# Fixed buffers for the transposed keys, and a finer last transfer, in a decode attention kernel

## The chip, the cores and the metric

The kernel runs on one core of a Trainium2 chip. The metric is the device time of one execution in microseconds (us); the medians, the lowest and the highest run are given. A profile has its own clock, the *span*, from the first to the last instruction of the core. The device time is a little longer than the span, and that little gets a name, *the time outside the span*.

TensorE does the matmuls (PE in the profile, PEld its weight loads), VectorE (DVE) the transposes and small vector work, ScalarE (ACT) activations, GpSimd (POOL) masks, and SyncE (SP) issues the loads.

## The reference, cut to what matters

```python
x = A_x                                        # [4, 1, 1024]
g = sigmoid((x * gate_w).sum(-1))
a = attention(x @ wq, k_cache, v_cache) @ wo   # 4 x 32 heads, 8192 keys of 128 each
b = x + sigmoid(x @ w_r) * ((silu(x @ w_gate) * (x @ w_up)) @ w_down)
return g * a + (1 - g) * b
```

There is one query per head. Keys and values are 268 MB each, every byte is used once, and nearly all of the time is their loading.

## The kernel before

Each step `u` handles two heads. A 4 MB piece of keys comes into one of five ring slots; VectorE transposes it in four chunks into a tile `T` from a pool of two; TensorE multiplies the chunk. The matching 4 MB piece of values comes eight steps later into the same ring and is read by TensorE only.

```python
ring = ctx.enter_context(tc.tile_pool(name="ring", bufs=5))
ttp = ctx.enter_context(tc.tile_pool(name="ttp", bufs=2))
# ... cut ...
def k_piece(u):
    # ... cut: the query's weights Z ...
    kn = slot()                                                # 128 rows of 32 KB
    nc.sync.dma_start(out=kn[:], in_=kv_view(A_k_cache, u))
    for c in range(JR // CJ):                                  # 4 chunks
        T = ttp.tile([P, CJ, 2, 32, 2], BF, name="T", tag="T")
        nc.vector.transpose(out=T[:].rearrange("p j h i e -> p (j h i e)").bitcast(U32),
                            in_=kn[:, c * CJ * Dh:(c + 1) * CJ * Dh].bitcast(U32))
        for he in range(4):
            for z in range(2):
                nc.tensor.matmul(sps[:, z, :], lhsT=Z[:, he, s:s + P], rhs=T[:, 16 * z:16 * z + 16, half, :, e], ...)
```

Dependencies are found by the framework, which also places the waits on semaphores. When a tile of the pool is used again, VectorE's new write waits for TensorE's last read of it and, besides, for VectorE's own earlier write.

At the end, after the last value piece, the output projection's weights `wo` come in 1 MB blocks; the last two blocks come in halves, and each half is multiplied as it lands:

```python
def wo_block(g, r0=0, r1=FR):                   # FR = 4 rows per partition, of 2 KB each
    # ... cut ...
    nc.sync.dma_start(out=w[:, r0:r1]..., in_=wov[:, g, r0:r1]...)
    def use():
        for r in range(r0, r1):
            for n in range(NH):                 # 2 matmuls a row
                mm_acc(acc[:, n * NB:(n + 1) * NB], LT[:, r, g, :], w[:, r, n * NB:(n + 1) * NB])
    return use
# ... cut ...
last += [wo_block(g, r, r + FR // 2) for g in (NWB - 2, NWB - 1) for r in (0, FR // 2)]
```

Of the kernel before, what the change touches and what calls it, by code (L numbers as in the profile page):

```python
# [9 lines left out]
BF = mybir.dt.bfloat16  # L10
F32 = mybir.dt.float32
U32 = mybir.dt.uint32
ACT = mybir.ActivationFunctionType
ALU = mybir.AluOpType
# [25 lines left out]
def kernel(  # L40
# [23 lines left out]
    nc = tc.nc  # L64
    P = 128
    Bn, Sq, D = A_x.shape
    _, H, Sk, Dh = A_k_cache.shape
    F = B_w_gate.shape[1]
    DT = D // P
# [10 lines left out]
    CJ = 32  # L80
    NT = Bn * H // HT
    LAG = GT
    FR = 4
# [9 lines left out]

    const = ctx.enter_context(tc.tile_pool(name="const", bufs=1))
    ring = ctx.enter_context(tc.tile_pool(name="ring", bufs=5))
    ttp = ctx.enter_context(tc.tile_pool(name="ttp", bufs=2))
    ptp = ctx.enter_context(tc.tile_pool(name="ptp", bufs=1))
    stat = ctx.enter_context(tc.tile_pool(name="stat", bufs=2))
    accp = ctx.enter_context(tc.tile_pool(name="accp", bufs=1, space=PSUM))
# [5 lines left out]
    def small(shape, dtype=F32):  # L105
        return mps.tile(shape, dtype, name="small", tag="small")

    def slot():
        return ring.tile([P, RING], BF, name="piece", tag="piece")


    NX = Bn + 2
    x6 = const.tile([NX, D], BF)
# [5 lines left out]
    acc4 = accp.tile([P, 2, 512], F32)  # L119
    o_ps = accp.tile([P, 2, 512], F32)  # L120
    q_ps = scp.tile([P, 2, 512], F32, name="S_ps")
# [15 lines left out]
    for he in range(4):  # L137
        half, e = divmod(he, 2)
# [48 lines left out]
    def mm_acc(out_ap, lhsT, rhs, start=False):  # L187
        nc.tensor.matmul(out_ap, lhsT=lhsT, rhs=rhs, start=start, stop=True, skip_group_check=True)  # L188
# [3 lines left out]

    def gates():
        rg_ps = small([P, 2, Bn])
        wrep = ttp.tile([P, 2, DT, P], BF, name="wrep", tag="T")
        for i in range(2):
            nc.vector.tensor_copy(out=wrep[:, i, :, :], in_=xw[:, :, Bn + i:Bn + i + 1].to_broadcast([P, DT, P]))
            for t in range(DT):
                nc.tensor.matmul(rg_ps[:, i, :], lhsT=wrep[:, i, t, :], rhs=xT[t], start=(t == 0), stop=(t == DT - 1))
        nc.scalar.activation(out=sgb[:], in_=rg_ps[:], func=ACT.Sigmoid)  # L200
        nc.vector.tensor_scalar(out=c12[:, 0, :], in0=sgb[:, 1, :], scalar1=-1.0, scalar2=1.0, op0=ALU.mult, op1=ALU.add)
        nc.vector.tensor_tensor(out=c12[:, 1, :], in0=c12[:, 0, :], in1=sgb[:, 0, :], op=ALU.mult)
        nc.vector.tensor_tensor(out=dg[:], in0=ident[0:Bn, 0:Bn], in1=c12[0:Bn, 0, :], op=ALU.mult)

    def add_x():
        xf = ttp.tile([Bn, D], F32, name="xf", tag="T")
        nc.vector.tensor_copy(out=xf[:], in_=x6[0:Bn])
        for n in range(NH):
            mm_acc(acc[:, n * NB:(n + 1) * NB], dg[:], xf[:, n * NB:(n + 1) * NB])

# [17 lines left out]
    def wq_piece(t0):  # L228
        w = slot()[:, :TW * H * Dh].rearrange("p (t n) -> p t n", t=TW)
        nc.sync.dma_start(out=w, in_=wqv[:, t0:t0 + TW, :])  # L230
        x_rows(q_ps, w, t0, H * Dh // NB)

    def q_done():
        qs = ttp.tile([P, 2, 4, P], BF, name="qs", tag="T")
        nc.vector.tensor_copy(out=qs[:].rearrange("p z c d -> p z (c d)"), in_=q_ps[:])
        qt = small([P, 2, 4, 4, 32], BF)
        for z in range(2):
            for c in range(4):
                nc.tensor.transpose(out=qt[:, z, c].rearrange("p k i -> p (k i)"), in_=qs[:, z, c, :], identity=identb[:])
            nc.vector.tensor_copy(out=qT[:, 16 * z:16 * z + 16, :].rearrange("p (k c) b -> p c k b", c=4),  # L240
                                  in_=qt[:, z, :, :, 0:Bn])
        qa_ps = small([P, 4, H * Bn])
        for he in range(4):
            nc.tensor.matmul(qa_ps[:, he, :], lhsT=R[:, he, :], rhs=qT[:].rearrange("p h b -> p (h b)"),
                             start=True, stop=True)
        nc.vector.tensor_copy(out=qa[:].rearrange("p e h b -> p e (h b)"), in_=qa_ps[:])
# [4 lines left out]
        x_rows((o_ps, acc4)[w_i], w, t0, FG)  # L251

    def h_done():
        h = ttp.tile([P, 2, 512], F32, name="h", tag="T")
        nc.scalar.activation(out=h[:], in_=o_ps[:], func=ACT.Silu)
        nc.vector.tensor_tensor(out=h[:], in0=h[:], in1=acc4[:], op=ALU.mult)
        for z in range(2):
            ht = small([P, FR, 4, 32])
            for r in range(FR):
                nc.tensor.transpose(out=ht[:, r].rearrange("p k i -> p (k i)"), in_=h[:, z, r:512:FR], identity=ident[:])  # L260
            kn = min(4, FG - 4 * z)
            for r in range(FR):
                nc.vector.tensor_tensor(out=hT[:, 4 * z:4 * z + kn, r, :], in0=ht[:, r, 0:kn, 0:Bn],
                                        in1=c12[:, 1:2, :].to_broadcast([P, kn, Bn]), op=ALU.mult)
# [12 lines left out]
    NWB = H // WB  # L277
# [13 lines left out]
    def wo_block(g, r0=0, r1=FR):  # L291

        home, at = divmod(g, 4)
        if home not in wo_home:
            wo_home[home] = slot().rearrange("p (g r n) -> p g r n", g=4, r=FR)
        w = wo_home[home][:, at]
        nc.sync.dma_start(out=w[:, r0:r1].rearrange("p r n -> p (r n)"),
                          in_=wov[:, g, r0:r1].rearrange("p r n -> p (r n)"))

        def use():  # L300
            for r in range(r0, r1):
                for n in range(NH):
                    mm_acc(acc[:, n * NB:(n + 1) * NB], LT[:, r, g, :], w[:, r, n * NB:(n + 1) * NB])
        return use
# [6 lines left out]
    def flush():  # L311
        while pending:
            pending.pop(0)()

    def heads(u):
        return divmod(u * HT, H)

    def kv_view(cache, u):
        b, h0 = heads(u)
        return cache[b, h0:h0 + HT].rearrange("h (r j) d -> (h r) (j d)", j=JR)  # L320

    def k_piece(u):
        b, h0 = heads(u)
        g, t = divmod(u, GT)
        Z = Zt[u % 2]
        nc.gpsimd.tensor_tensor(out=Z[:, :, 31:31 + P].rearrange("p e (s d c) -> p e s d c", s=HT, d=QH)[:, :, :, :, 0],  # L326
                                in0=qa[:, :, h0:h0 + HT, b:b + 1].to_broadcast([P, 4, HT, QH]),
                                in1=mq[:].rearrange("p o (s d) -> p o s d", s=HT).to_broadcast([P, 4, HT, QH]), op=ALU.mult)
        if t == 0:
            S_ps[g] = scp.tile([P, 2, 512], F32, name="S_ps")  # L330
        sps = S_ps[g]
        kn = slot()
        nc.sync.dma_start(out=kn[:], in_=kv_view(A_k_cache, u))
        for c in range(JR // CJ):
            T = ttp.tile([P, CJ, 2, 32, 2], BF, name="T", tag="T")
            nc.vector.transpose(out=T[:].rearrange("p j h i e -> p (j h i e)").bitcast(U32),  # L336
                                in_=kn[:, c * CJ * Dh:(c + 1) * CJ * Dh].bitcast(U32))
            s = 31 - (JT * t + c)
            for he in range(4):
                half, e = divmod(he, 2)  # L340
                for z in range(2):
                    nc.tensor.matmul(sps[:, z, :], lhsT=Z[:, he, s:s + P], rhs=T[:, 16 * z:16 * z + 16, half, :, e],  # L342
                                     start=(t == 0 and c == 0 and he == 0),
                                     stop=(t == GT - 1 and c == JT - 1 and he == 3))
            if c == 0:
                flush()
        if t == GT - 1:
            softmax(g)
# [35 lines left out]
    def v_piece(u):  # L384
# [31 lines left out]
        def finish():  # L416
# [8 lines left out]


    gates()
    wq_piece(0)
    wq_piece(TW)
    q_done()  # L430
    side = [lambda: gu_piece(wgv, 0, 0), lambda: gu_piece(wgv, 0, TW), lambda: gu_piece(wuv, 1, 0),
            lambda: (gu_piece(wuv, 1, TW), h_done()), lambda: wd_piece(0, 4), lambda: wd_piece(4, FG - 4)]
    GE = NWB - RH // WB
    order = []
# [3 lines left out]
    for kind, u in order:  # L438
        if kind == "k":
            k_piece(u)  # L440
        if (kind, u) == ("v", NT - 1):
            for g in range(2):
                wo_block(g)()
        if kind == "v":
            v_piece(u)
        if side and (kind == "v" or u < LAG):
            side.pop(0)()
        if (kind, u) == ("k", NT // 2):
            add_x()
        if (kind, u) == ("v", NT - RT):  # L450
            o_rows(0, GE)
    last = [wo_block(g) for g in range(2, NWB - 2)]
    last += [wo_block(g, r, r + FR // 2) for g in (NWB - 2, NWB - 1) for r in (0, FR // 2)]
    last.pop(0)()
    flush()
    last.pop(0)()
# [38 lines left out]
```

## Time and profile before

| | before |
|---|---|
| device time, median of 3 (lowest to highest) | 1349.41 us (1349.39 to 1349.46) |
| span of the profiled run | 1347.8 us |
| moved | 576.2 MB at a mean 428 GB/s |
| busy: TensorE, VectorE | 79%, 47% |

From the page of the kernel before: the row of DMA busy tenths and of GB/s in 40 slices of the span, then two of the queues (packets, MB, share of the 16 DMA engines' span).

```profile
DMA  9999999999999999999999999999999999999997
GB/s 403 433 433 422 433 430 430 432 433 430 430 433 430 430 431 434 429 431 432 433 428 432 433 430 430 433 431 429 432 434 429 428 433 434 429 428 434 432 423 323
...
q1 hardware_dynamic: 22104, 575.68, 99.5%
q8 instruction: 27, 0.44, 0.1%
```

The loads never pause: 9 in every slice but the last. This kernel is bound by its loads.

Next, the view of line 336, the key transposes, before. The last number of a waiting line is how often.

```profile
L336 DVE STREAM_TRANSPOSE T<-piece x256: 2253/2271/2314, 33.1 to 1232.9; 128x2048 uint32<-128x2048 uint32 x128
L336 DVEq EVENT_SEMAPHORE  x230: 21/21/50, 35.5 to 1230.8; - x115
its engine sat idle before it (us, times) until:
  DMA piece<-in_A_k_cache_dram: 321.1, 45
  PE S_ps L342: 106.4, 62
  PE o_ps L401: 9.1, 1
```

VectorE's idle time before a transpose is ended by a load or by TensorE, never by VectorE itself. The second row is the waits that did not fit into a transpose and became instructions of their own, of 21 ns. (The `x115` at its end, as the `x128` of the first row, is the view's count of forms.)

Two rows of VectorE's timeline before (start, us, what). The four transposes of the first row, by the order of instructions, carry the wait on VectorE itself; the two of the second do not.

```profile
611.51 8.89 DVE L336 STREAM_TRANSPOSE T<-piece 128x2048 uint32<-128x2048 uint32 x4 [8.33 <-DMA piece<-in_A_k_cache_dram]
...
636.50 4.44 DVE L336 STREAM_TRANSPOSE T<-piece 128x2048 uint32<-128x2048 uint32 x2
```

Both come to 2.22 us a transpose.

The end of the chain that ended last, before: start, us, what.

```profile
1328.82 14.95 DMA piece<-in_A_wo_dram
1343.77 0.04 issue
1343.81 1.04 PE acc L188 x4
1344.85 0.02 issue
1344.87 0.57 ACT res L463
```

The last load lands at 1343.77, four matmuls take 1.04 us, then come the casts and the stores.

### The profile page before, as it was taken

How to read it: one execution, taken by the hardware profiler on the slowest of the kernel's cores; microseconds unless marked ns; L12 is line 12 of the kernel's file. 1: busy time of each engine (PE TensorE's matmuls, PEld its weight loads, DVE VectorE, ACT ScalarE, POOL GpSimd, SP SyncE). 2: the span in 40 equal slices, each digit the busy share in tenths (PEclk: the TensorE clock that was granted, in tenths of full speed). 3: DMA queues.
4: the chain of work that ended last, by engine and by line, in shares of the span. 5: the costliest groups of instructions: out<-in, count | busy, mean ns of one | idle time of the engine just before them, and what ended most of it. 6: DMA issues, size and time to landing. Idle time of an engine off the chain costs nothing.

```text
span 1347.8 us, 8253 instructions
## 1 busy us (share of the span) xinstructions
PE 1059.3 (79%) x4600; PEld 233.2 (17%) x2412; DVE 631.4 (47%) x375; ACT 41.5 (3%) x46; POOL 47.9 (4%) x115
## 2 busy tenths in 40 slices
PE   2667779876978868876998769888788859797878
PEld 0111111211111111111212111211112112121111
DVE  3555755535544554454545454444544456346000
ACT  0000010001000010001000010000000010000000
POOL 2000000000000000000000000000000000000000
PEclk8878989898989989989898879899888979999899
DMA  9999999999999999999999999999999999999997
GB/s 403 433 433 422 433 430 430 432 433 430 430 433 430 430 431 434 429 431 432 433 428 432 433 430 430 433 431 429 432 434 429 428 433 434 429 428 434 432 423 323
DMA packets 22162, 576.22 MB, mean 428 GB/s; under 512 B 2399, under 2 KB 2407, under 8 KB 2925
## 3 DMA queue, kind: packets, MB, share of 16 engines
q1 hardware_dynamic: 22104, 575.68, 99.5%
q8 instruction: 27, 0.44, 0.1%
q14 instruction: 11, 0.08, 0.0%
q10 hardware_dynamic: 20, 0.02, 0.0%
HBM read 575.68 MB, written 0.01 MB: 427 GB/s over the span
## 4 chain that ended last, share of the span: by engine, by line
DMA 50%; PE 30%; DVE 11%; issue 6%; ACT 1%; POOL 1%; SPq 0%; DVEq 0%; ACTq 0%
DMA piece<-in_A_k_cache_dram 40%; PE o_ps L401 16%; PE S_ps L342 13%; DVE T L336 10%; DMA piece<-in_A_v_cache_dram 9%; PE small L419 1%; DMA piece<-in_A_wo_dram 1%; POOL PB L373 1%; DVE PT L367 1%; ACT PTs L365 1%; ACT OS L411 1%; DVE OS L412 1%; POOL tot L377 0%; PE acc L188 0%; PE o_ps L225 0%
## 5 line engine op out<-in xcount | busy, mean ns | idle before, releaser
L336 DVE STREAM_TRANSPOSE T<-piece 128x2048 uint32<-128x2048 uint32 x256 | 576.1, 2288 | 437.0 <-DMA piece<-in_A_k_cache_dram 321.1
L342 PE MATMUL S_ps<-T,Z 128*128 128x512 bf16 x2048 | 544.6, 416 | 246.6 <-DVE T L336 235.3
L401 PE MATMUL o_ps<-piece,PB 128*16 128x512 bf16 x2048 | 457.6, 382 | 14.8 <-DMA piece<-in_A_v_cache_dram 14.8
L342 PEld LDWEIGHTS <-Z 128*128 128x128 bf16 x1024 | 108.0, 105 | 667.2 <-issue 664.3
L401 PEld LDWEIGHTS <-PB 128*16 128x16 bf16 x1024 | 91.9, 90 | 373.1 <-issue 361.3
L412 DVE SCALAR_TENSOR_TENSOR OS<-o_ps,mE,OS 128x512 f32<-128x512 f32 x16 | 12.0, 751 | 174.6 <-ACT OS L411 174.6
L326 POOL TENSOR_TENSOR Z<-qa,mq 128x16 bf16<-128x16 bf16 x64 | 16.7, 262 | 1072.3 <-PE S_ps L342 1054.3
L411 ACT ACTIVATE OS<-o_ps,mE 128x512 f32<-128x512 f32 x16 | 11.0, 687 | 1040.5 <-PE o_ps L401 1040.5
L419 PEld LDWEIGHTS small<-selg,OS 128*128 128x128 f32 x128 | 24.9, 273 | 12.2 <-issue 11.1
L419 PE MATMUL small<-selg,OS 128*128 128x8 f32 x128 | 22.3, 302 | 0.0
L353 DVE TENSOR_REDUCE m<-S_ps 128x1 f32<-128x1024 f32 x8 | 9.8, 1225 | 15.9 <-PE S_ps L342 15.9
L188 PE MATMUL acc<-piece,LT 128*4 128x512 bf16 x64 | 14.9, 378 | 1.7 <-DMA piece<-in_A_wo_dram 1.6
L373 POOL COPY PB<-PT 64x1024 bf16<-64x1024 bf16 x8 | 15.1, 1884 | 29.1 <-DVE rex L375 29.1
L372 ACT COPY PB<-PT 64x1024 bf16<-64x1024 bf16 x8 | 15.3, 1908 | 10.6 <-DVE PT L367 10.6
L367 DVE STREAM_TRANSPOSE PT<-PTs 128x1024 bf16<-128x1024 bf16 x8 | 10.0, 1245 | 11.9 <-ACT PTs L365 11.9
L188 PE MATMUL acc<-piece,hT 128*4 128x512 bf16 x56 | 12.4, 379 | 0.0
L131 PE MATMUL small<-identb,x 6*128 6x6 bf16 x8 | 0.6, 194 | 14.2 <-DVE identb L128 14.2
L379 DVE RECIPROCAL rinv<-tot 128x16 f32<-128x16 f32 x8 | 2.0, 253 | 19.9 <-POOL tot L377 19.9
L365 ACT ACTIVATE PTs<-S_ps,negm 128x1024 bf16<-128x1024 f32 x8 | 8.9, 1113 | 70.0 <-DVE negm L362 70.0
L225 PE MATMUL S_ps<-piece,xw 128*4 128x512 bf16 x64 | 6.6, 591 | 3.0 <-DMA piece<-in_A_wq_dram 3.0
L422 DVE SCALAR_TENSOR_TENSOR OT<-small,sgb,rinv 128x8 bf16<-128x8 f32 x16 | 3.2, 202 | 11.7 <-PE small L419 11.7
L358 POOL PARTITION_ALL_REDUCE gmx<-mex x8 | 3.1, 390 | 81.9 <-issue 50.3
(72 smaller groups left out, 74.6 us busy)
## 6 DMA issues: line engine op xcount, KB each, us to landing
piece<-in_A_k_cache_dram SPq DMA_DIRECT2D x64, 4096.0 KB, 39.4
piece<-in_A_v_cache_dram SPq DMA_DIRECT2D x63, 4096.0 KB, 39.1
piece<-in_A_wq_dram SPq DMA_DIRECT2D x2, 4096.0 KB, 22.1
piece<-in_B_w_gate_dram SPq DMA_DIRECT2D x2, 3584.0 KB, 40.1
piece<-in_B_w_up_dram SPq DMA_DIRECT2D x2, 3584.0 KB, 34.6
piece<-in_A_wo_dram SPq DMA_DIRECT2D x6, 1024.0 KB
piece<-in_B_w_down_dram SPq DMA_DIRECT2D x1, 4096.0 KB, 35.6
piece<-in_A_v_cache_dram SPq DMA_DIRECT2D x4, 1024.0 KB, 32.6
```

The lines of the kernel that those rows point to most:

```text
L188: nc.tensor.matmul(out_ap, lhsT=lhsT, rhs=rhs, start=start, stop=True, skip_group_check=True)
L326: nc.gpsimd.tensor_tensor(out=Z[:, :, 31:31 + P].rearrange("p e (s d c) -> p e s d c", s=HT, d=QH)[:, :, :, :, 0], in0=qa[:, :, h0:h0 + HT ...
L336: nc.vector.transpose(out=T[:].rearrange("p j h i e -> p (j h i e)").bitcast(U32), in_=kn[:, c * CJ * Dh:(c + 1) * CJ * Dh].bitcast(U32))
L342: nc.tensor.matmul(sps[:, z, :], lhsT=Z[:, he, s:s + P], rhs=T[:, 16 * z:16 * z + 16, half, :, e], start=(t == 0 and c == 0 and he == 0), ...
L365: nc.scalar.activation(out=PTs[:], in_=sps[:].rearrange("p z n -> p (z n)"), func=ACT.Exp, bias=negm[:, 0:1], scale=scale, accum_out=rs[:, ...
L367: nc.vector.transpose(out=PT[:].rearrange("p j i -> p (j i)"), in_=PTs[:])
L372: nc.scalar.copy(out=Bv[0:W, :, :, 0, :], in_=Pv[0:W])
L373: nc.gpsimd.tensor_copy(out=Bv[W:P, :, :, 1, :], in_=Pv[W:P])
L401: nc.tensor.matmul(o_ps[row:row + NM, e, :], lhsT=B_[:, JT * t + c, z, w].rearrange("p e s j -> p (e s j)"), rhs=vn[:, j0 * Dh:(j0 + 4) * ...
L411: nc.scalar.activation(out=o_sb[:], in_=o_ps[:, 0, :], func=ACT.Copy, scale=mE[:, 0:1])
L412: nc.vector.scalar_tensor_tensor(out=o_sb[:], in0=o_ps[:, 1, :], scalar=mE[:, 1:2], in1=o_sb[:], op0=ALU.mult, op1=ALU.add)
L419: nc.tensor.matmul(oT[:, :], lhsT=o_sb[:, q * Dh:(q + 1) * Dh], rhs=selg[:, q].rearrange("p t s -> p (t s)"), start=(q == 0), stop=(q == 3))
```

## The change

Its intent is twofold: take away VectorE's waits on itself (two fixed buffers, and a declaration to the framework that a transpose need not wait for the one two before it, because that one's readers are waited for anyway), and shorten the work behind the last load (the last block in three transfers, the last of one row per partition). Core of the diff; the other users of the old pool were moved to the fixed buffers in the same way and are cut:

```diff
-    ttp = ctx.enter_context(tc.tile_pool(name="ttp", bufs=2))
+    Tt = [const.tile([P, CJ * P], BF, name=f"T{i}") for i in range(2)]
+    turned = []
+
+    def turn(in_ap):
+        T = Tt[len(turned) % 2]
+        i = nc.vector.transpose(out=T[:].bitcast(U32), in_=in_ap.bitcast(U32)).ins
+        if len(turned) >= 2:
+            tc.declare_no_dep(i, turned[-2], reason="its readers are waited for")
+        turned.append(i)
+        return T[:].rearrange("p (j h i e) -> p j h i e", j=CJ, h=2, i=32)
...
-            T = ttp.tile([P, CJ, 2, 32, 2], BF, name="T", tag="T")
-            nc.vector.transpose(...)
+            T = turn(kn[:, c * CJ * Dh:(c + 1) * CJ * Dh])
...
-    last += [wo_block(g, r, r + FR // 2) for g in (NWB - 2, NWB - 1) for r in (0, FR // 2)]
+    last += [wo_block(NWB - 2, 0, 2), wo_block(NWB - 2, 2, 4)]
+    last += [wo_block(NWB - 1, 0, 2), wo_block(NWB - 1, 2, 3), wo_block(NWB - 1, 3, 4)]
```

More of the change, by code (lines that the diff above doesn't have):

```diff
@@ L194, in gates @@
         rg_ps = small([P, 2, Bn])
-        wrep = ttp.tile([P, 2, DT, P], BF, name="wrep", tag="T")
+        wrep = Tt[0][:, 0:2 * DT * P].rearrange("p (w t d) -> p w t d", w=2, t=DT)
         for i in range(2):
@@ L205, in add_x @@
     def add_x():
-        xf = ttp.tile([Bn, D], F32, name="xf", tag="T")
-        nc.vector.tensor_copy(out=xf[:], in_=x6[0:Bn])
+        xf = Tt[len(turned) % 2][0:Bn, 0:2 * D].bitcast(F32)
+        nc.vector.tensor_copy(out=xf, in_=x6[0:Bn])
         for n in range(NH):
@@ L233, in q_done @@
     def q_done():
-        qs = ttp.tile([P, 2, 4, P], BF, name="qs", tag="T")
-        nc.vector.tensor_copy(out=qs[:].rearrange("p z c d -> p z (c d)"), in_=q_ps[:])
+        qs = Tt[1][:, 0:1024].rearrange("p (z c d) -> p z c d", z=2, c=4)
+        nc.vector.tensor_copy(out=qs.rearrange("p z c d -> p z (c d)"), in_=q_ps[:])
         qt = small([P, 2, 4, 4, 32], BF)
@@ L253, in h_done @@
     def h_done():
-        h = ttp.tile([P, 2, 512], F32, name="h", tag="T")
-        nc.scalar.activation(out=h[:], in_=o_ps[:], func=ACT.Silu)
-        nc.vector.tensor_tensor(out=h[:], in0=h[:], in1=acc4[:], op=ALU.mult)
+        h = Tt[len(turned) % 2][:, 0:2048].bitcast(F32).rearrange("p (z n) -> p z n", z=2)
+        nc.scalar.activation(out=h, in_=o_ps[:], func=ACT.Silu)
+        nc.vector.tensor_tensor(out=h, in0=h, in1=acc4[:], op=ALU.mult)
         for z in range(2):
@@ L334, in k_piece @@
         for c in range(JR // CJ):
-            T = ttp.tile([P, CJ, 2, 32, 2], BF, name="T", tag="T")
-            nc.vector.transpose(out=T[:].rearrange("p j h i e -> p (j h i e)").bitcast(U32),
-                                in_=kn[:, c * CJ * Dh:(c + 1) * CJ * Dh].bitcast(U32))
+            T = turn(kn[:, c * CJ * Dh:(c + 1) * CJ * Dh])
             s = 31 - (JT * t + c)
```

## The prediction

> **What bounds the kernel.** The loads do. The page counts 576.2 MB at a mean 428 GB/s over a span of 1347.8 us; its DMA row shows 9 in every slice but the last, and in windows of 10 us the sixteen DMA engines are busy 0.95 to 1.05 of the time from 10 to 1330 us, without a gap. [...] VectorE is busy 47%, TensorE 79%, both fed by the loads. The queue is deep: a 4 MB piece lands 39 us after its issue, though it takes 9.8 us at 428 GB/s, so some four are in flight.
>
> **What the change removes.** By the order of instructions, 239 of the 256 key transposes wait on VectorE's own semaphore before; three do after. Waits on TensorE and the loads stay. I expect almost nothing:
> - The waits view lists as enders of VectorE's idle time before transposes only the key loads (321.1 us), the score matmuls (106.4) and the value matmuls (9.1): never VectorE. The own wait is for a transpose two back, long done.
> - Four transposes that carry it run in 8.89 us; two that don't, in 4.44 us: 2.22 us each. [...]
> - 115 separate semaphore instructions of 21 ns go, 2.4 us in sum, on an engine half idle.
> - Were a transpose 0.1 us earlier, its slot would go back 0.1 us earlier to a queue holding some 30 us of work: off the critical path.
>
> The order on TensorE and of the loads before the tail is unchanged.
>
> **The tail.** After the last load (1343.8 us) come four matmuls (1.04 us), casts (0.6) and stores. The change leaves two matmuls behind the last piece; at the trace's 0.21 us a matmul and 0.38 for the last, about 0.6 us: 0.43 us saved. Against it: one more transfer, with rows of 2 KB for 4 KB. The DMA rate falls before the end (246, 207, 45 GB/s in windows of 2 us from 1338), so some DMA engines finish up to 5 us before the last; the split doesn't mend that. [...] Tail transfers wait at issue for a semaphore used eight transfers before (27.3 us of such waits): the new last one waits for a wo piece landing near 1331 us, 12 us before the end, so the queue shouldn't run dry.
>
> **Predicted time:** 1348.9 us, 0.3 to 0.5 below before; 8 in 10: 1346.8 to 1350.6. Faster by over 2%: 0.005; within 2%: 0.99; slower by over 2%: 0.005.
>
> **What would show it.** Right: mean 427 to 429 GB/s; transposes still 2.22 us apart, with the same enders of idle time, each within 10 us of now; separate semaphore instructions on VectorE near zero; two matmuls after the last load, about 0.6 us; the last load ending within 1 us of 1343.8. Wrong: a gap in the DMA row, another DMA rate, or TensorE's wait for transposes (235.3 us) falling by tens of us with the span following.
>
> **What would make it wrong.** Drift of the load rate between runs [...]; the last transfer issued late or landing slowly on a lagging DMA engine; own waits hiding a cost that the view puts down to TensorE.

The forecast's sum came to 0.3 to 0.5 us saved, 1348.9 us. Of its two terms, the 0.43 us saved in matmuls stands; the other, an allowance against it for the extra transfer, was a guess without a number of the trace behind it. That the loads bound the kernel rests on the measured DMA row and rate, and that the own waits cost nothing on the measured 2.22 us a transpose with and without them.

## The result, and the profile after

| | before | after |
|---|---|---|
| device time, median of 6 (lowest to highest) | 1349.40 us (1349.26 to 1349.46) | 1349.52 us (1349.23 to 1349.70) |
| span of the profiled run | 1347.8 us | 1347.4 us |
| ratio, 95% interval | | 1.0001, 0.9988 to 1.0014 |

A ratio is the mean time of one kernel's fast runs over that of the other's fast runs of the same rounds, so it is not quite the ratio of the medians. The expected third to half of a microsecond is missing, and the two rows of the table disagree: the span is 0.4 us shorter, the device time is not. Which of the two is right is the question of the experiments.

First, the profile after. From the page of the changed kernel:

```profile
DMA  9999999999999999999999999999999999999997
...
q1 hardware_dynamic: 22248, 575.68, 99.5%
q8 instruction: 27, 0.44, 0.1%
```

The view of the key transposes, now line 117:

```profile
L117 DVE STREAM_TRANSPOSE T<-piece x256: 2253/2271/2312, 32.8 to 1233.0; 128x2048 uint32<-128x2048 uint32 x128
L117 DVEq EVENT_SEMAPHORE  x49: 21/21/50, 51.7 to 1224.9; - x49
its engine sat idle before it (us, times) until:
  DMA piece<-in_A_k_cache_dram: 309.9, 42
  PE S_ps L352: 122.4, 65
  PE acc L200: 3.2, 1
```

The separate waits fell from 230 to 49. The idle time before transposes is what it was (435.5 us by these rows, 436.6 before), some 10 us of it moved from loads to TensorE. VectorE's timeline after:

```profile
611.40 8.89 DVE L117 STREAM_TRANSPOSE T<-piece 128x2048 uint32<-128x2048 uint32 x4 [9.40 <-DMA piece<-in_A_k_cache_dram]
...
636.71 4.44 DVE L117 STREAM_TRANSPOSE T<-piece 128x2048 uint32<-128x2048 uint32 x2
```

To the hundredth of a microsecond the same. The end of the chain after:

```profile
1326.22 16.20 DMA piece<-in_A_wo_dram
1342.42 0.04 issue
1342.46 1.91 PE acc L200 x8
1344.37 0.02 issue
1344.40 0.57 ACT res L474
```

TensorE now runs the last eight matmuls of `wo` without a pause, and is done at 1344.37 in place of 1344.85. The completion records in the trace put the landing of the very last load at 1343.73, against 1343.77 before: the loads end where they ended, and the work behind them is 0.6 us in place of 1.1. So within the span the tail did just what was predicted. The chain shows one thing more: it runs through the landing of the transfer before the last (1342.42), not of the last. TensorE came from six matmuls straight to its last two at 1343.77, 0.04 us after the last landing, so here the last load and TensorE's own work end together, and no run shows that a still finer split would gain anything.

### The profile page after: what moved, and what is told of

Its sections match the earlier page's. It is cut to its first block, busy times and chain, and to the rows that moved or that the text cites. A ratio compares the mean times of both kernels' runs of the same rounds, so it can differ in the third digit from the quotient of the medians.

```text
span 1347.4 us, 8079 instructions
## 1 busy us (share of the span) xinstructions
PE 1065.2 (79%) x4600; PEld 234.8 (17%) x2412; DVE 631.7 (47%) x375; ACT 41.5 (3%) x46; POOL 48.0 (4%) x115
## 4 chain that ended last, share of the span: by engine, by line
DMA 48%; PE 30%; DVE 17%; issue 2%; ACT 1%; POOL 1%; SPq 0%; DVEq 0%; ACTq 0%
DMA piece<-in_A_k_cache_dram 41%; DVE T L117 15%; PE o_ps L411 14%; PE S_ps L352 14%; DMA piece<-in_A_v_cache_dram 5%; DMA piece<-in_A_wo_dram 1%; PE small L429 1%; POOL PB L383 1%; ACT PTs L375 1%; DVE PT L377 1%; DVE OS L422 1%; ACT OS L421 0%; DVE m L363 0%; PE acc L200 0%; POOL tot L387 0%
## 5 line engine op out<-in xcount | busy, mean ns | idle before, releaser
L117 DVE STREAM_TRANSPOSE T<-piece 128x2048 uint32<-128x2048 uint32 x256 | 576.2, 2288 | 436.0 <-DMA piece<-in_A_k_cache_dram 309.9
L338 POOL TENSOR_TENSOR Z<-qa,mq 128x16 bf16<-128x16 bf16 x64 | 16.8, 263 | 1072.7 <-PE S_ps L352 1053.2
L200 PE MATMUL acc<-piece,hT 128*4 128x512 bf16 x56 | 12.4, 379 | 0.0
```

What stands on the lines that cost most here:

```text
L117: i = nc.vector.transpose(out=T[:].bitcast(U32), in_=in_ap.bitcast(U32)).ins
L200: nc.tensor.matmul(out_ap, lhsT=lhsT, rhs=rhs, start=start, stop=True, skip_group_check=True)
L338: nc.gpsimd.tensor_tensor(out=Z[:, :, 31:31 + P].rearrange("p e (s d c) -> p e s d c", s=HT, d=QH)[:, :, :, :, 0], in0=qa[:, :, h0:h0 + HT ...
```

## The experiments

Eleven experiments were run. The differences below are of a few tenths of a microsecond, and the 95% interval of a ratio is about 0.0013 wide to each side (1.8 us), so no interval alone separates them. What does is that the runs of one kernel on one chip mostly scatter by 0.2 to 0.4 us, and that the ranges in question don't overlap; where they do, nothing is claimed.

### The two halves of the change, alone

The changed kernel again, then the fixed buffers with the old tail, then the new tail with the old pool, all on one chip. The edits are the two hunks above, one at a time.

> The changed kernel once more, beside its two halves on one chip. Theory (loads bound it; the own waits cost nothing; the tail split shortens the span by about 0.4 us): ratio to before 0.9995 to 1.0003. Rival (the two halves pull against each other): the ratio is also near 1, but the halves alone differ from 1 in opposite directions by over 0.0005.

> Fixed buffers alone, the tail as before. Theory: ratio 1.0000 within 0.0004; idle time of VectorE before key transposes by the same enders within 15 us of 437; span about 1347.8 us with the last load landing near 1343.8. Rival (own waits cost time, the new tail gives it back): 0.5 us or more below before.

> The three-transfer tail alone, with the pool and its own waits. Theory: the span falls by 0.3 to 0.5 us as in the profile of the changed kernel (1347.4 after 1347.8), the timed ratio 0.9996 to 1.0001. Rival (the extra transfer costs what the shorter last step saves): ratio 1.0000 or above.

| kernel (5 runs each, before 9) | device time, median (range) | span, median | outside the span (range) |
|---|---|---|---|
| before | 1349.40 us (1349.28 to 1349.59) | 1347.7 us | 1.66 to 1.76 us |
| both | 1349.40 us (1349.30 to 1349.52) | 1347.4 us | 2.00 to 2.10 us |
| fixed buffers alone | 1349.71 us (1349.64 to 1349.95) | 1347.7 us | 2.01 to 2.09 us |
| new tail alone | 1349.12 us (1349.07 to 1349.22) | 1347.4 us | 1.67 to 1.74 us |

The last column is device time less span, run by run. By their numbers all three theories held: the ratios are 1.0000, 1.0003 and 0.9998, and the rival's halves, over 0.0005 from 1, are not there. But in device time the halves have opposite signs, as the rival written for the first run had it, and each range lies clear of that of the kernel before. The tail alone gains 0.28 us of device time, all of it within the span. The fixed buffers alone lose 0.31 us, none of it within the span: there the view of their transposes shows 46 waits for loads and 62 for TensorE (45 and 62 before), and the last load lands at 1343.83. They make the time *outside* the span 0.34 us longer. Together they cancel. That is where the expected gain went.

### How far VectorE is from the critical path

Before asking why, the prediction's main claim was tested by making VectorE much slower. After each key transpose of the kernel before, one more of half the size:

```diff
+            nc.vector.transpose(out=xd[:].bitcast(U32),
+                                in_=kn[:, c * CJ * Dh:c * CJ * Dh + CJ * Dh // 2].bitcast(U32))
```

> The kernel before with one more transpose of half size after every key transpose, 256 in all, results unused; at about half of 2.22 us each, some 290 us more work on VectorE (47% busy to about 68%). Theory (VectorE is off the critical path, behind a queue of loads some 30 us deep): the time stays within 0.2%, DMA row 9 throughout. Rival (VectorE's pace reaches the time through the give-back of key slots): longer by a few per cent, up to 20%.

It took 1349.45 us (1349.24 to 1349.54, 4 runs), against 1349.40 before. From its page, first part and groups:

```profile
PE 1030.6 (76%) x4600; PEld 228.4 (17%) x2412; DVE 914.3 (68%) x631; ACT 41.6 (3%) x46; POOL 48.0 (4%) x115
...
L339 DVE STREAM_TRANSPOSE xd<-piece 128x1024 uint32<-128x1024 uint32 x256 | 308.0, 1203 | 0.0
```

308 us of added work on VectorE cost nothing that can be measured. So a change that saves VectorE a few microseconds of work cannot be expected to shorten the span.

### Does the own wait cost anything where the loads do not bound?

Both kernels (with the old tail) with thin loads: each key piece loads half its bytes and uses them twice, each value piece a quarter. The sums differ from the reference's; the comparison with the reference passed all the same, so it is not a fine one.

```diff
-        nc.sync.dma_start(out=kn[:], in_=kv_view(A_k_cache, u))
+        nc.sync.dma_start(out=kn[:, 0:RING // 2], in_=kv_view(A_k_cache, u)[:, 0:RING // 2])
...
-        for c in range(JT):        # value matmuls
+        for c in range(1):
```

> A wrong result on purpose: each key piece loads half of its bytes and uses them twice, each value piece loads and multiplies a quarter; pool and own waits as before. The loads fall to about 216 MB, 505 us at 428 GB/s, so VectorE (576 us of key transposes) and TensorE bound it: I expect 620 to 720 us. It is the reference point for the next run: does the own wait cost time where VectorE is the bound?

> The same thin loads with fixed buffers, without the own waits. Theory (the own wait is for a transpose two back, long done, and costs nothing even where VectorE bounds): within 0.3% of the run with the pool, key transposes still 2.22 us apart in a row. Rival (own waits cost tens of ns each, hidden so far behind the loads): faster by 239 times 20 to 100 ns, 5 to 24 us, 1 to 4%.

Both ran slower than the 620 to 720 us that I had expected, 835.65 us (834.58 to 836.67) with the pool and 833.57 us (832.53 to 838.12) with fixed buffers, 4 runs each: VectorE was 75% busy and TensorE 81%, so neither bounds the run alone. The medians are 0.25% apart and the ranges overlap, so the total leaves open a cost of 2 us; the 5 to 24 us of the rival are not there. The timelines answer directly. Pool, then fixed buffers:

```profile
397.96 6.65 DVE L336 STREAM_TRANSPOSE T<-piece 128x2048 uint32<-128x2048 uint32 x3
405.88 6.70 DVE L336 STREAM_TRANSPOSE T<-piece 128x2048 uint32<-128x2048 uint32 x3 [1.27 <-PE S_ps L342]
```

```profile
399.66 6.66 DVE L117 STREAM_TRANSPOSE T<-piece 128x2048 uint32<-128x2048 uint32 x3
407.58 6.70 DVE L117 STREAM_TRANSPOSE T<-piece 128x2048 uint32<-128x2048 uint32 x3 [1.27 <-PE S_ps L352]
```

In the run with the pool the first and the third of each three carry the own wait (by the semaphores in the trace; 191 of its 256 transposes do, against 3 with fixed buffers). Three in a row take 6.65 to 6.70 us with and without it. It has no cost that these rows show.

### What lengthens the time outside the span

The fixed-buffer kernels differ from the others in one thing that has nothing to do with buffers: VectorE's program is shorter, because 175 separate waits are gone from it. To tell the two apart, first 256 copies of one element were added to the fixed-buffer kernel with the old tail, then only 16 to the changed kernel. The cut below is of the second; the first has the copy after every transpose.

```diff
+            if c == 0 and u % 4 == 0:                    # 16 copies; without this line 256
+                nc.vector.tensor_copy(out=xd[:], in_=kn[:, 0:1])
```

> Fixed buffers with the old tail, and 256 copies of one element added on VectorE (results unused). In the runs so far, the device time exceeds the span of the trace by 1.70 us with the pool (before, the tail alone, the loaded VectorE) and by 2.05 us with the fixed buffers. Theory L (that part depends on how many instructions VectorE's program has: 614 records before, 692 in the loaded one, 439 with fixed buffers, about 695 here): back to 1.70 us. Theory B (it comes with the fixed buffers themselves): stays at 2.05 us. The span stays at 1347.7 within 0.3 us in both.

> The changed kernel with only 16 one-element copies added on VectorE. The device time exceeded the span by 2.05 us in every run whose VectorE program has 439 records (changed kernel, fixed buffers alone, all weight loads), and by 1.70 us at 454 (thin loads with fixed buffers), 614, 689 and 692. Theory L (the length of VectorE's program decides, with a step between 439 and 454): at about 455 records back to 1.70 us outside the span, the span 1347.4 as in the changed kernel, so 1349.1 us, 0.3 below both kernels. Rival (what the 256 copies or the thin loads did to timing inside the span brought it back): stays 2.05 us, 1349.4.

Fixed buffers with 256 copies took 1349.30 us (1349.11 to 1349.41), against 1349.46 (1349.25 to 1349.60) before on the same chip; their span, 1347.6 us, is that of the fixed buffers alone within 0.1, and the time outside it is back to 1.71: theory L. Put in order of the number of VectorE's instruction records in the trace, over all runs:

| kernel | VectorE records | outside the span (range) |
|---|---|---|
| changed (first measurement; again) | 439 | 2.03 to 2.10; 2.00 to 2.10 us |
| fixed buffers alone | 439 | 2.01 to 2.09 us |
| all weight loads (next section) | 439 | 2.01 to 2.09 us |
| half of the value matmuls (next section) | 439 | 2.01 to 2.10 us |
| the probe (last experiment, one run) | 439 | 2.01 us |
| changed with 16 copies | 450 | 1.67 to 1.72 us |
| thin loads, fixed buffers | 454 | 1.68 to 1.75 us |
| before (36 runs), new tail alone | 614 | 1.66 to 1.78 us |
| thin loads, pool | 616 | 1.68 to 1.77 us |
| fixed buffers with 256 copies | 689 | 1.70 to 1.74 us |
| VectorE loaded | 692 | 1.69 to 1.74 us |

No kernel falls between. Fixed buffers stand on both sides, so it is not the buffers; TensorE's weight loads run from 1644 to 4600 over these kernels without an effect on it. Eleven idle instructions more on VectorE (16 copies, less five waits that they made needless) take 0.35 us off. All kernels on the long side have the same 439 records on VectorE, though, so what is shown is that instructions added to this program take the 0.35 us away; where the border lies, and whether any shorter program is on the long side too, is not shown. What happens there lies outside the profiled span, so no run shows the mechanism.

The changed kernel with 16 copies took 1348.99 us (1348.69 to 1349.07), against 1349.37 (1349.19 to 1349.51) before on the same chip: 0.38 us less, and the ranges do not overlap. That is what the change was meant to give. The changed kernel did not run on this chip; on the others it took what the kernel before took. The new tail alone gives most of this without any filler, 0.28 us on its own chip.

### What sets the last six microseconds

The prediction noted that some DMA engines finish up to 5 us before the last and left it there. A transfer over all partitions leaves 16 completion marks in the trace, as many as the page counts DMA engines; I take them as one for each. These are the marks of a 512 KB `wo` transfer at the end, in us (the trace does not say which engine is which):

```
before    1336.0 1336.1 1336.3 1337.2 1337.4 1337.7 1338.1 1340.7 1340.7 1340.8 1340.9 1341.0 1342.0 1342.1 1342.2 1342.5
```

At 22 us, one of the first transfers had all its marks within 1.2 us. The engines drift apart during the run although the load records of 32 KB after the start all but agree: median 1.215 us, 99 of 100 at most 1.225. What breaks the pace are the 27 fetches of 16 KB in queue q8, each about 1.06 us, and behind nearly each fetch one load record that takes about 0.5 us more. TensorE's 4600 matmuls and 2412 weight loads are 260 for each fetch, and in the two experiments below the number of fetches follows TensorE's program: 2188 weight loads more bring 9 more (256 instructions for each fetch), 1536 instructions less bring 6 fewer (261). The two thin kernels, with 4708 instructions, have 18 (262). VectorE's records went from 614 to 439 with the change, and the fetches stayed 27. So I take them to fetch TensorE's instructions.

The bookkeeping can be checked. Each fetch should push its DMA engine back by its own time and by the slow record behind it. In the trace of the kernel before, fetch records of q8 sum to 28.6 us, the 8 KB ones of q14 to 3.2, and the excess of the slow load records to 16.5: 48.4 us. The marks above lag the first of them by 55.6 us in sum, the early transfer's by 6.5: a growth of 49.2.

Two kernels changed the number of fetches. The first keeps the repeated weight loads that the kernel normally drops; the second drops half of the value matmuls (a different sum) and none of the loads.

```diff
-    nc.at_finalize(keep_weights)                        # all weight loads
```

```diff
-        for c in range(JT):                             # half of the value matmuls
+        for c in range(JT // 2):
```

> The changed kernel without its pass that drops repeated weight loads: 2048 or so more weight loads on TensorE (some 4000 of 97 ns in place of about 2400). Theory F (the fetching of TensorE's instructions, 27 transfers of 16 KB in the page's instruction queue, runs on the same DMA engines as the loads and pushes back the one that it falls on; the slowest of the 16 sets the end): some 8 to 16 more such transfers, the landing of a late transfer spread over more than the 6.3 us between its first and last DMA engine, and the time longer by 0.5 to 4 us. Rival (the spread has another cause): transfers more, but spread and time unchanged within 0.3 us.

> The changed kernel with all its loads, but only half of the value matmuls (a different sum on purpose): 1024 matmuls and 512 weight loads fewer on TensorE. Theory F (instruction fetches push back single DMA engines, the slowest sets the end): about 21 fetch transfers in place of 27, a spread of a late transfer's landing below 6.3 us, and the span 0.5 to 3 us shorter than 1347.4, although the bytes loaded are the same. Rival 1 (TensorE's work is on the critical path): tens of us shorter. Rival 2 (loads alone set the end, fetches don't matter): within 0.3 us of the changed kernel.

The instruction queue on the page of the first, then of the second:

```profile
q8 instruction: 36, 0.59, 0.2%
```

```profile
q8 instruction: 21, 0.34, 0.1%
```

| | fetches in q8 | fetches and slow records, sum | growth of the lag, sum | first to last mark | last load lands |
|---|---|---|---|---|---|
| half of the value matmuls | 21 | 38.7 us | 38.1 us | 4.9 us | 1342.22 |
| changed | 27 | 47.1 us | 46.1 us | 6.3 us | 1343.73 |
| all weight loads | 36 | 61.2 us | 60.1 us | 7.8 us | 1345.11 |

The sums agree within 2 us in all ten loads-bound traces for which I worked them out. With the same bytes to load, the last load lands 1.5 us earlier or 1.4 us later as the fetches go. The first mark of that last transfer does not move with them (1337.4, 1337.5 and 1337.4 us, in the order of the table): it is not that all loads run earlier or later, only the late DMA engines do. For all weight loads the span follows: 1348.9 us against 1347.4, device time 1350.93 us (1350.84 to 1350.99).

For half of the value matmuls my expected span was a miss: 1348.4 us median (device time 1350.48, 1348.18 to 1350.71), longer and not shorter, though its loads end earlier. One of its five runs, with a span of 1346.1 us, met the expectation of 0.5 to 3 us below 1347.4; the trace kept is of another, with 1348.7. The windows of that trace's tail show why: us, busy us of each engine, granted TensorE clock, DMA share, GB/s.

```profile
1326.00:1328.00 2.00, 0.00 (x0) 0.00 (x0) 0.00 (x0) 0.00 (x0) 0.00 (x0) 1.00 1.01 422
1328.00:1330.00 2.00, 0.29 (x1) 0.00 (x0) 0.00 (x0) 0.00 (x0) 0.00 (x0) 0.59 0.99 414
1330.00:1332.00 2.00, 2.00 (x6) 0.38 (x3) 0.00 (x0) 0.00 (x0) 0.00 (x0) 0.50 1.01 422
...
1338.00:1340.00 2.00, 2.00 (x25) 0.60 (x20) 0.19 (x1) 0.00 (x0) 0.00 (x0) 0.85 0.64 252
...
1342.00:1344.00 2.00, 2.00 (x11) 0.40 (x5) 0.00 (x0) 0.00 (x0) 0.00 (x0) 1.00 0.00 0
```

and its timeline in the same stretch:

```profile
1322.26 1.89 PE L411 MATMUL o_ps<-piece,PB 128*16 128x512 bf16 x8 [0.47 <-DMA piece<-in_A_v_cache_dram]
1329.71 3.57 PE L200 MATMUL acc<-piece,LT 128*4 128x512 bf16 x8 [5.57 <-DMA piece<-in_A_wo_dram]
1333.21 1.88 PE L429 MATMUL small<-selg,OS 128*128 128x8 f32 x8
1335.02 3.57 PE L200 MATMUL acc<-piece,LT 128*4 128x512 bf16 x8
...
1338.54 7.08 PE L200 MATMUL acc<-piece,LT 128*4 128x512 bf16 x32
```

With less to do, TensorE stood idle for 5.57 us; its granted clock was 0.50 when the tail's matmuls came, eight of them, and then eight more, took 3.57 us in place of 1.89, and it worked through the backlog until 1345.63, 3.4 us after the last load. The two slow groups cost 3.4 us together, as much as the backlog. The clock's 0.85 between 1338 and 1340 us, with 0.50 in the windows before and 1.00 after, puts its return at 1338.6 by my estimate, 8.9 us after TensorE took up work at 1329.71. In the kernel before the clock in these windows is 1.00, and TensorE was busy for 2.00 of the 2.00 us from 1326 to 1328, where it is idle here. My reading is that the work taken off TensorE, though off the critical path by its time, had kept the clock up for the matmuls that are on it. The trace of the kernel before fits it: all 35 stretches at a granted clock of 0.50 up to TensorE's last matmul begin at most 5.1 us after the start of an idle stretch of TensorE of 2.5 to 11.3 us, and all seven idle stretches of over 9 us are followed by 10.2 to 13.7 us at 0.50. But no run changes the idle time alone, so for the tail only the order of events in one trace is shown: the idle stretch, the clock of 0.50, the late end.

### A probe that disturbed what it measured

The last experiment was to learn which partitions belong to the slow DMA engines: one value piece in six transfers of 1, 2, 4, 8, 1 and 112 partitions.

> The changed kernel with the last but one value piece loaded in six transfers of 1, 2, 4, 8, 1 and 112 partitions, to see how the loads of a core are spread over its DMA engines: how many completion marks each of the six leaves, and when, against the 16 of a full transfer. The first DMA engine gets 12 rows in place of 8 if each transfer starts at the same engine, 1.2 us each, so the last load moves by 4.8 us less that engine's lead over the slowest (0 to 6.3 us): if it is a fast one, the end hardly moves; if it is a slow one, it comes 4 to 5 us later. If the assignment rotates, the end stays within 1 us.

A single run took 1366.21 us (state unknown), 16.8 us longer than before. Between 1300 and 1330 us the loads moved 193 to 230 GB/s in place of 420 and more. In that stretch a load record of 32 KB took a median 2.51 us in place of 1.215. The transfers of 1, 2, 4 and 8 partitions left one mark each some 0.4 us after their issue, and then 1, 2, 4 and 8 more: it looks as if a narrow transfer runs on that many DMA engines. The whole value piece issued just before them left its 16 marks over 12.4 us (1298.0 to 1310.4), and SyncE, waiting for that semaphore, issued nothing from 1295.1 to 1310.5. Neither of my two outcomes can be read from it. Which engine is the slow one, and whether the 3 us between the mean engine and the last could be won by giving it less at the end, stays open.

## Why the prediction was right, and where it was off

- **What bounds the kernel:** right. The loads' row is 9 in every slice but the last before and after, and 308 us more on VectorE cost nothing.
- **The own waits cost nothing:** right, within the span. 2.22 us a transpose with and without, also where the loads do not bound.
- **Separate waits, 115, to near zero:** off twice. 115 was the view's count over every second instruction; the line had 230, of which 49 remain. It did not matter to the time by way of VectorE.
- **Enders of idle time within 10 us:** missed by a little. Loads went from 321.1 to 309.9, TensorE's score matmuls from 106.4 to 122.4; the sum stayed.
- **The tail:** right. The last load lands at 1343.73 (predicted within 1 us of 1343.8), 0.6 us of matmuls follow, and TensorE ends 0.48 us earlier; the queue did not run dry. The new tail alone gives 0.28 us of device time.
- **The predicted time, 1348.9 us, "0.3 to 0.5 below before":** inside the range, but the gain is missing: 0.12 above in the first measurement (the ranges overlap), 0.00 in the second. The range is 3.8 us wide, so no change at all would have lain in it too, and that it held says little. The step that failed is unspoken: I added changes of the span and took the rest of the device time for constant. The term that was set to zero measured 0.34 us: the time outside the span grew when VectorE's program shrank from 614 records to 439, and that ate the tail's gain. Why it grew stays open.
- **Uneven DMA engines, "the split doesn't mend that":** right, and no more than noticed. Their drift comes from instruction fetches and costs the last load about 3 us against an even spread (55.6 us of lag over 16 engines is 3.5 us on average, against 6.5 for the last).

## What to carry to other kernels

In a kernel bound by its loads, look at what runs after the last load lands, not at waits of engines that the loads feed; a wait for something long done cost nothing here, where the loads bound (2.22 us a transpose with and without it) and where they did not (6.65 to 6.70 us for three in a row). When effects are below a microsecond, measure device time beside the span and each half of a change alone: two halves can cancel, and one of them may act where the profile does not look. And a long unrolled program is itself a load: here the fetches of 16 KB, one for 256 to 262 of TensorE's instructions, fell on the DMA engines that carry the data, and with 36, 27 and 21 of them the last load landed at 1345.11, 1343.73 and 1342.22 us. In four of the five runs of the last kernel the time did not follow: in the one traced, TensorE stood idle for 5.57 us just before the tail, and the tail began at a granted clock of 0.50.
